# Packed attention and a squared-ReLU layer on one core: values by nine tokens per partition, W_out by four rows per partition

## The chip, the cores and the metric

The kernel runs on one core of a Trainium2 chip. The core's engines run side by side and wait for each other by semaphores: PE (TensorE) does matmuls from the SBUF into the PSUM, DVE (VectorE) and ACT (ScalarE) work on elements of both memories, POOL (GpSimd) works on the SBUF and issues DMAs here, SP (SyncE) issues DMAs. The metric is the device time of one execution in microseconds; lower is better.

## The reference

Inputs are q, k and v of 8 batches x 8 heads x 576 tokens x 64, packed queries p of 32 tokens per head, W_in of 512x2048 and W_out of 2048x512, all float32.

```python
def sm_attn(qq, kk, vv):
    s = scale * np.matmul(qq, kk.transpose(0, 1, 3, 2))
    s = s - np.max(s, axis=-1, keepdims=True)
    a = np.exp(s)
    a = a / (np.sum(a, axis=-1, keepdims=True) + 1e-09)
    return np.matmul(a, vv)
p_packed = sm_attn(p, k, v)                  # 32 packed tokens per head
out = sm_attn(q, p_packed, p_packed)         # back to 576 tokens per head
x = out.transpose(0, 2, 1, 3).reshape(B * S, H * D)
h = x @ w_in
g = np.maximum(h, 0.0) ** 2
return g @ w_out                             # 4608 x 512
```

## The kernel before

**The work.** Each batch is done in two attention steps and two layers. The 8 heads of a batch are two groups of four (qd 0 and 1), each with 4 x 32 = 128 packed tokens on the partitions. First attention: scores `s1` of the 32 packed tokens of each head against 576 keys, negative maximum `m1` on DVE, exponential `x1` with its sums on ACT into `e1` (128 x 576 per group), turned by PE (`eT`) in pieces of 128 columns into PSUM, copied out (`eo`), and multiplied with the values (`pv`). `rd` and `pp` divide by the sums, `pt`/`po` and `bd`/`bs` turn the result. Second attention: scores `s2`, turned (`t2`), maximum `m2`, subtraction `sb`, exponential `x2`, sums `su`, division `a2`, turned (`aT`) to `a2T`. As the values of the second attention are the packed result, W_in is multiplied by it first: `w0` to `w3` give the product with W_in for one batch in four quarters of 512 columns, copied from PSUM by `W0` to `W3` into the tile `wp`. Then come the layers: `h` multiplies one block of 128 hidden features with half of a batch's tokens (288 columns, two matmuls; batches 0 and 1 are cut into 256 and 320), `r` is the ReLU from PSUM, `q` the square of two blocks into `gT`, `o` two of the 16 matmuls of 128 tokens by 512 columns with W_out, `c` the copy of a finished tile of 128 tokens to the SBUF, `d` its store.

**The order.** All of it stands in one string, ORDER, whose words are issued one after the other: `h3.0.11` is batch 3, half 0, block 11; `r3.0.11:a` its ReLU on ACT (`:v` DVE, `:p` POOL, DVE where nothing stands); `o12.4` the fifth pair of tile 12; `eT41` batch 4, group 1; `Lk`, `Lv`, `Lq` load keys, values and queries, `Wi` and `Wo` the weights. Each engine takes its own words in this order and waits only for the results and buffers that it needs. So the place of a DVE word among PE words means nothing by itself; its place among DVE words does. Loads of inputs and weights are issued by POOL, stores by SP, each queue in order of its words.

**Buffers around the change.** [...] A bank comes free when its ReLU or copy is done. `e1` is a single buffer for both groups. Finished tiles have five buffers (`op`); a buffer comes free when its store is done.

**What the change touches** (lines of the profile). `setup` (L192 to L195) makes three value buffers `v_b` and two `v_end`, the latter cleared. For batches 2 to 7 `load_v` (L313 to L320) issues two DMAs per group: 512 tokens, four neighbouring tokens per partition, into `v_b`; and the 64 that are left into one half of the partitions of `v_end`. `st_exp1` (L439) writes `e1` in the order of the tokens. `st_e1T` (L461) turns four pieces of every fourth column per group, and in group 1 a fifth with the last 64 tokens of group 0 and the first 64 of group 1. `st_pv` (L488) multiplies: per batch four matmuls for that fifth piece, with 128 columns (L500), and 32 with 64 columns (L507), all with 128 rows and 32 columns of the array. Batches 0 and 1 have another form (three tokens per row piece, 96 rows) and keep it. `load_w_out` (L263) loads a quarter of W_out so that partition p of block fb holds row 128 fb + p. `st_wp_out` (L626) copies a quarter of `wp` with its columns in order.

Of the kernel before, what the change touches and what calls it, by code (L numbers as in the profile page):

```python
# [12 lines left out]
BF16 = mybir.dt.bfloat16  # L13
# [55 lines left out]
h1.1.12 r1.1.0:a bd2 pt2 qT20 o4.7 bs2:a Lk40 h1.1.5 po2:v r1.1.12:a o5.7 q1.1.0:v c4:a h1.1.10 r1.1.5:v c5:a s22 d4
r1.1.10:v h1.1.4 o6.0 t221 r1.1.4:a h1.1.9 d5 o7.0 q1.1.2:a t220 h1.1.13 r1.1.9:a o6.1 qT30 r1.1.13:a Lq4 h1.1.11  # L70
q1.1.4:a m221 w22 w32 r1.1.11:a o6.2 m220 W32:a h1.1.14 h1.1.15 W22:v Lv31 o6.3 r1.1.14:a q1.1.6:a o7.1 o6.4 sb21:v
r1.1.15:a Lv40 o7.2 q1.1.5:a kT30 o7.3 q1.1.7:a o7.4 sb20:v Lk41 x221 o6.5 qT31 o7.5 x220 o6.6 su21 o6.7 o7.6 su20 c6:a
o7.7 w02 a221:v c7:a d6 w12 o8.0 W02:a a220:v o8.1 d7 o8.2 aT21 W12:a o8.3 aT20 o8.4 Lq5 h2.0.1 h2.0.0 r2.0.1:v o8.5
r2.0.0:a o8.6 q2.0.0:v h2.0.2 h2.0.3 r2.0.2:v o9.0 Lk50 o8.7 r2.0.3:v h2.0.5 c8:a s13 q2.0.1:v r2.0.5:a h2.0.4 d8 m130
o10.0 r2.0.4:a h2.0.6 kT40 h2.0.7 r2.0.6:a o10.1 r2.0.7:a q2.0.2:v h2.0.10 Lk51 x130 m131 o9.1 h2.0.8 r2.0.10:a q2.0.3:v
o9.2 r2.0.8:a kT41 h2.0.13 x131 eT30 h2.0.9 r2.0.13:v o10.2 eo30:a rd3 r2.0.9:v h2.1.1 eT31 q2.0.4:v h2.0.14 r2.1.1:a
o10.3 r2.0.14:v eo31:a h2.0.11 Lk61 o9.3 r2.0.11:v o9.4 h2.0.12 h2.1.5 q2.0.5:v r2.0.12:a pv3 r2.1.5:v h2.0.15 q2.0.6:v
h2.1.4 pp3 r2.0.15:a o9.5 r2.1.4:v h2.1.6 bd3 pt3 q2.0.7:v h2.1.0 bs3:a o9.6 r2.1.6:v r2.1.0:v Lv41 po3:a o9.7 q2.1.2:v
h2.1.8 q2.1.0:v c9:a h2.1.2 r2.1.8:v s23 r2.1.2:a Lv50 d9 o11.0 t230 h2.1.3 h2.1.7 t231 o10.4 r2.1.3:a w23 m230 r2.1.7:a
w03 W23:a h2.1.10 q2.1.1:v h2.1.9 q2.1.3:v o10.5 W03:a m231 o10.6 o11.1 sb30:v r2.1.10:a o11.2 r2.1.9:a sb31:v o10.7  # L80
x230 o11.3 q2.1.4:v c10:a h2.1.15 qT40 o11.4 x231 h2.1.11 su30 r2.1.15:a w13 d10 r2.1.11:a w33 W13:a h2.1.14 su31
h2.1.13 o12.0 r2.1.14:a a230:v o12.1 r2.1.13:a o12.2 W33:a q2.1.5:v o12.3 a231:v h2.1.12 o11.5 aT30 r2.1.12:a o12.4 aT31
o12.5 q2.1.6:v q2.1.7:v h3.0.5 h3.0.2 qT41 r3.0.5:a o12.6 h3.0.0 r3.0.2:v Lq6 o11.6 r3.0.0:a o12.7 h3.0.1 h3.1.1
r3.0.1:v c12:a o11.7 r3.1.1:v s14 d12 c11:a q3.0.0:v h3.0.4 kT50 h3.0.3 r3.0.4:a o13.0 r3.0.3:a m140 d11 h3.0.9 Lk60
o14.0 r3.0.9:a q3.0.1:v h3.1.3 x140 kT51 h3.1.0 o14.1 r3.1.3:a m141 o13.1 Lk70 r3.1.0:a h3.0.8 q3.0.2:v eT40 x141 h3.0.7
r3.0.8:v o13.2 eo40:v r3.0.7:a h3.0.6 q3.1.0:v o14.2 q3.0.4:v r3.0.6:a eT41 rd4 q3.0.3:v h3.0.11 eo41:a h3.1.2 r3.0.11:v
o14.3 r3.1.2:v o13.3 h3.0.12 h3.0.10 q3.1.1:v pv4 r3.0.10:a r3.0.12:v o14.4 Lv51 pp4 h3.0.13 q3.0.5:v h3.0.14 r3.0.13:a
bd4 o13.4 r3.0.14:v bs4:a pt4 Lv60 q3.0.6:v h3.0.15 h3.1.8 o13.5 po4:v r3.1.8:a o14.5 r3.0.15:v s24 q3.0.7:v h3.1.11
t240 h3.1.6 r3.1.11:a o13.6 t241 r3.1.6:a o13.7 w04 qT51 c13:a w14 h3.1.4 W04:a m241 o16.0 d13 h3.1.5 m240 r3.1.4:a
o16.1 r3.1.5:a o14.6 W14:a sb41:v h3.1.9 h3.1.7 q3.1.2:v o14.7 r3.1.7:a sb40:v r3.1.9:a w24 w34 x241 q3.1.3:v h3.1.10  # L90
c14:v o16.2 W34:a h3.1.13 q3.1.4:v d14 o15.0 su41 r3.1.10:a o16.3 x240 o15.1 r3.1.13:v W24:a h3.1.12 q3.1.5:v o16.4
a241:v o15.2 r3.1.12:a h3.1.14 su40 h3.1.15 o16.5 r3.1.14:a q3.1.6:v o15.3 r3.1.15:a a240:v o15.4 o16.6 q3.1.7:v o15.5
aT40 aT41 o16.7 qT50 o15.6 c16:a h4.0.1 h4.0.4 Lq7 r4.0.1:v o15.7 d16 r4.0.4:v o17.0 c15:a h4.0.3 h4.0.2 r4.0.3:v o17.1
# [20 lines left out]
r6.0.4:v o26.1 qT70 x171 h6.0.0 h6.0.2 d25 o26.2 r6.0.0:v r6.0.2:a rd7 eT70 q6.0.0:v h6.0.14 eo70:v h6.0.9 r6.0.14:a
o26.3 r6.0.9:v h6.0.5 o27.0 r6.0.5:v h6.0.6 eT71 q6.0.2:v r6.0.6:a h6.0.11 o26.4 eo71:v r6.0.11:a h6.0.3 q6.0.5:v h6.1.1
pv7 r6.1.1:v o26.5 r6.0.3:a pp7 o26.6 q6.0.1:v h6.0.7 bd7 h6.1.5 pt7 o27.1 bs7:v r6.1.5:a r6.0.7:a o26.7 po7:v q6.0.3:v
h6.0.15 c26:a h6.0.8 w07 w27 r6.0.15:v W07:a d26 o28.0 W27:v h6.1.0 o27.2 r6.0.8:a r6.1.0:a o28.1 q6.0.7:v o27.3
q6.0.4:v q6.1.0:v h6.0.12 h6.1.6 r6.0.12:v o28.2 o28.3 r6.1.6:v h6.0.13 o27.4 h6.1.7 r6.0.13:v s27 r6.1.7:a o27.5
# [16 lines left out]
class Kernel:  # L135
# [42 lines left out]
    def setup(self):  # L178
# [15 lines left out]
        for x in self.v_end:  # L194
            nc.vector.memset(x, 0.0)  # L195
# [673 lines left out]
```

## Time and profile before

| | |
|---|---|
| median of three runs | 240.62 us (240.46 to 240.88) |
| the profiled execution | 240.85 us, of which 239.1 us are the span from the first to the last instruction |
| busy, share of the span | PE 230.8 us (97%), DVE 200.4 (84%), ACT 143.9 (60%), POOL 73.0 (31%) |
| DMA | 28.50 MB in 31868 packets, 119 GB/s over the span |

Times are in microseconds, means of one instruction in nanoseconds. A row of a group gives line, engine, operation, output and inputs, shapes and count; behind the first bar the busy time and the mean of one instruction; behind the second the engine's idle time just before these instructions and what ended it. PE's instructions overlap: a matmul's duration includes its way through the array, and the next starts before it ends, so what one costs in a row of equal ones is the distance of their starts. The chain is followed back from the last instruction, at each step to what released it; its shares add up to the span. A window's row has one column per engine: busy time and number of instructions, then the granted clock of TensorE and the DMA's share. A row of waits names who waited for whom, the sum, the number of waits and the longest.

### The profile page before, as it was taken

To read this page: it belongs to the slowest core of one execution; us is meant where nothing else is said; L and a number is where in the kernel's file an instruction comes from. 1 tells how busy PE (TensorE), PEld (TensorE's weight loads), DVE (VectorE), ACT (ScalarE), POOL (GpSimd) and SP (SyncE) were. 2 spreads that over 40 slices of the span, in tenths; PEclk is the share of its full clock that TensorE was granted. 3 is DMA by queue.
4 is the path that set the end of the run, shared out by engine and by line. 5 is a ranking of instruction groups with operands and counts; after the bars stand their busy time and mean duration, and the time that the engine had idled before them with its cause. 6 is when DMAs were issued, how large, how long until landed. Compare 5 with 4: busy or idle time off the path is not lost.

```text
span 239.1 us, 5971 instructions
## 1 busy us (share of the span) xinstructions
PE 230.8 (97%) x2355; PEld 123.5 (52%) x2355; DVE 200.4 (84%) x455; ACT 143.9 (60%) x311; POOL 73.0 (31%) x122
## 2 busy tenths in 40 slices
PE   8887999999999999999999999999999999999994
PEld 2444553456544564456545654565545644555543
DVE  2779986998997889989998889997899789987740
ACT  2348974887896657775683648774485346732300
POOL 8509782785664661054203340002000000000000
PEclk9999999999999999999999999999999999999999
DMA  6999999999999979169923993216112112111224
GB/s 109 193 200 213 200 206 204 161 243 211 199 203 217 192 106 143 44 91 197 127 64 45 195 129 60 47 44 96 45 27 67 47 44 46 44 47 44 49 59 111
DMA packets 31868, 28.50 MB, mean 119 GB/s; under 512 B 8161, under 2 KB 26337, under 8 KB 31841
## 3 DMA queue, kind: packets, MB, share of 16 engines
q0 software_dynamic: 25312, 18.55, 53.7%
q1 hardware_dynamic: 6384, 9.51, 14.9%
q8 instruction: 18, 0.29, 0.5%
q10 hardware_dynamic: 144, 0.07, 0.1%
q14 instruction: 10, 0.07, 0.1%
HBM read 37.22 MB, written 9.44 MB: 195 GB/s over the span
## 4 chain that ended last, share of the span: by engine, by line
PE 92%; DVE 5%; ACT 1%; issue 0%; ACTq 0%
PE ps_o L694 52%; PE ps_h L637 26%; PE ps_s L411 3%; PE ps_wp L623 3%; PE ps_idle L341 3%; PE ps_e1T L474 2%; PE ps_pv L507 1%; DVE r L644 1%; DVE sums L591 1%; ACT qT L457 1%; DVE wp L459 0%; PE ps_pv L500 0%; DVE a2T L613 0%; DVE gT L682 0%; DVE s L563 0%; PE ps_o L699 0%
## 5 line engine op out<-in xcount | busy, mean ns | idle before, releaser
L694 PE MATMUL ps_o<-w_out_bf,gT 128*128 128x512 bf16 (+1 forms) x576 | 147.0, 378 | 0.0
L637 PE MATMUL ps_h<-a2T,wp 128*128 128x288 bf16 (+2 forms) x512 | 89.9, 286 | 1.5 <-ACT wp L457 0.7
L642 ACT ACTIVATE r<-ps_h 128x288 bf16<-128x288 f32 (+2 forms) x161 | 61.4, 413 | 48.7 <-PE ps_h L637 44.0
L694 PEld LDWEIGHTS <-gT 128*128 128x128 bf16 x576 | 54.5, 98 | 43.9 <-issue 3.4
L637 PEld LDWEIGHTS <-wp 128*128 128x128 bf16 x512 | 47.5, 98 | 42.8 <-issue 7.7
L644 DVE TENSOR_SCALAR r<-ps_h 128x288 bf16<-128x288 f32 (+2 forms) x95 | 41.3, 449 | 11.8 <-PE ps_h L637 10.7
L682 DVE TENSOR_TENSOR gT<-r 128x576 bf16<-128x576 bf16 (+2 forms) x108 | 46.5, 444 | 2.3 <-ACT r L642 1.4
L457 ACT CAST wp<-ps_wp 128x1024 bf16<-128x1024 f32 (+1 forms) x31 | 29.2, 961 | 9.1 <-PE ps_wp L623 9.1
L457 ACT COPY o_sb<-ps_o 128x512 f32<-128x512 f32 x26 | 15.2, 590 | 12.3 <-PE ps_o L694 12.0
L271 POOL DMA_DIRECT2D q_b<-in_q_dram x16 | 10.9, 685 | 29.1 <-DVE qT L369 25.2
L319 POOL DMA_DIRECT2D v_b<-in_v_dram x12 | 9.3, 779 | 32.3 <-PE ps_pv L507 30.4
L271 POOL DMA_DIRECT2D k_b<-in_k_dram x28 | 15.3, 550 | 12.1 <-DVE kT L357 5.0
L451 ACT ACTIVATE e<-ps_s,nm 128x576 bf16<-128x576 f32 x16 | 11.8, 743 | 7.1 <-DVE nm L437 7.1
L357 DVE STREAM_TRANSPOSE kT<-k_b 128x576 uint32<-128x576 uint32 x16 | 12.3, 770 | 2.9 <-DMA k_b<-in_k_dram 2.9
L341 PE MATMUL ps_idle<-gT 128*128 128x512 bf16 (+1 forms) x34 | 11.4, 465 | 1.2 <-DVE gT L190 1.2
L437 DVE TENSOR_REDUCE nm<-ps_s 128x1 f32<-128x576 f32 x16 | 11.5, 740 | 1.1 <-PE ps_s L411 1.1
L369 DVE STREAM_TRANSPOSE qT<-q_b 128x576 uint32<-128x576 uint32 (+2 forms) x16 | 10.8, 683 | 2.0 <-DMA q_b<-in_q_dram 2.0
L680 ACT ACTIVATE gT<-r 128x640 bf16<-128x640 bf16 (+1 forms) x18 | 12.2, 694 | 0.4 <-DVE r L644 0.2
L591 DVE TENSOR_REDUCE sums<-e 128x18 f32<-128x576 f32 (+2 forms) x20 | 12.1, 604 | 0.0
L585 ACT ACTIVATE e<-d 128x576 f32<-128x576 f32 (+2 forms) x20 | 11.7, 600 | 0.6 <-DVE d L579 0.6
L579 DVE TENSOR_TENSOR d<-s,mx 128x576 f32<-128x576 f32 (+2 forms) x19 | 11.7, 641 | 0.0
L573 DVE TENSOR_REDUCE mx<-s 128x18 f32<-128x576 f32 (+2 forms) x20 | 11.6, 609 | 0.0
(68 smaller groups left out, 175.5 us busy)
## 6 DMA issues: line engine op xcount, KB each, us to landing
out_dram<-o_sb SPq DMA_DIRECT2D x65, 128.0 KB, 2.4
v_b<-in_v_dram POOLq DMA_DIRECT2D x12, 256.0 KB, 5.6
w_out_bf<-in_moe_w_out_dram POOLq DMA_DIRECT2D x4, 512.0 KB, 10.7
q_b<-in_q_dram POOLq DMA_DIRECT2D x6, 288.0 KB, 6.2
q_b<-in_q_dram POOLq DMA_DIRECT2D x12, 144.0 KB, 6.9
k_b<-in_k_dram POOLq DMA_DIRECT2D x12, 108.0 KB, 4.7
gT<-in_v_dram POOLq DMA_DIRECT2D x4, 288.0 KB, 7.9
w_in_bf<-in_moe_w_in_dram POOLq DMA_DIRECT2D x4, 256.0 KB, 10.7
```

The costliest lines, as they stand in the source:

```text
L271: engine.dma_start(x[n:], s[:P - n])
L341: self.nc.tensor.matmul(ps[:, :m], lhsT=self.nought[:, :P], rhs=self.nought[:, :m], start=True, stop=True)
L357: self.nc.vector.transpose(t["kT"][:].rearrange("p s e -> p (s e)").bitcast(U32), t["k"][:].rearrange("p t d -> p (t d)").bitcast(U32))
L451: self.nc.scalar.activation(out, x, ACT.Exp, bias=t["nm"], accum_out=self.den[b][:, qd:qd + 1])
L457: engine.copy(out, x)
L591: nc.vector.reduce_sum(out=sums[:, x], in_=t["e2"][:, x], axis=AX.X)
L637: self.nc.tensor.matmul(ps, lhsT=self.att[b, 0]["wp"][:, qd, fb * P:(fb + 1) * P], rhs=self.att[b, qd]["a2T"][:, s0:s1], start=(qd == 0), ...
L642: engine.activation(r, ps, ACT.Relu)
L644: engine.tensor_scalar_max(r, ps, 0.0)
L680: engine.activation(out, r, ACT.Square)
L682: engine.tensor_tensor(out=out, in0=r, in1=r, op=ALU.mult)
L694: self.nc.tensor.matmul(self.o[tt][:, e], lhsT=self.gT[:, fb, a:a + P], rhs=self.w_out_bf[:, fb, e], start=(i == 0), stop=(i == self.NFB - 1))
```

## The change

Three things change, for batches 2 to 7 where nothing else is said.

- **Values.** Tokens go nine per partition: group 0's four heads lie on partitions 0 to 63, group 1's on 64 to 127, loaded by one DMA per group into one of two buffers (by the batch's parity). The exponentials of both groups are written into one row of 9 x 128 columns, so that piece j holds, for both groups, the tokens 9p + j; one exponential thereby writes every second column. `eT` of group 0 turns pieces 0 to 4, that of group 1 pieces 5 to 8, and each piece holds both groups. `pv_tiles` does 72 matmuls per batch on tiles of 64 rows and 32 columns, the two groups into two PSUM banks. `v_end` and its clearing go.
- **W_out.** Each quarter is loaded with four neighbouring rows per partition. Hidden features are permuted to match: the copy of `wp` from PSUM reads every fourth column, for all batches.
- **The order.** From the twelfth `h` of batch 1 on the same words stand in another order, and part of them on another engine: squares 59 on DVE and 49 on ACT (98 and 10 before), ReLUs 71 and 142 (81 and 132), W copies 4 and 20 (2 and 22), `bs` 4 and 2 (2 and 4). Loads and stores are issued in another order too.

```diff
-        self.v_b = [self.consts.tile([P, QH, 4, D], BF16, name=f"v_b{i}") for i in range(3)]
-        self.v_end = [self.consts.tile([P, QH, self.NQ, D], BF16, name=f"v_end{i}") for i in range(2)]
-        for x in self.v_end:
-            nc.vector.memset(x, 0.0)
+        self.v_b = [self.consts.tile([P, QH, T // 2, D], BF16, name=f"v_b{i}") for i in range(2)]
...
-            self.w_out_bf[:, f0:f1, :], self.w_out[f0 * P:f1 * P].rearrange("(fb p) e -> p fb e", p=P))
+            self.w_out_bf[:, f0:f1, :], self.w_out[f0 * P:f1 * P].rearrange("(p fb) e -> p fb e", p=P))
...
-        o, r = (D, 0) if qd else (0, 4 * P)
-        self.nc.gpsimd.dma_start(x, s[:, o:o + 4 * P].rearrange("h (p j) d -> p h j d", j=4))
-        self.nc.gpsimd.dma_start(y[qd * D:(qd + 1) * D, :, qd, :], s[:, r:r + D].rearrange("h p d -> p h d"))
+        x = t["v"] = self.v_b[b % 2][qd * D:(qd + 1) * D]
+        self.nc.gpsimd.dma_start(x, s.rearrange("h (p j) d -> p h j d", j=T // 2))
...
-            out = e1.rearrange("p (l a u) -> p l a u", a=2, u=T // 2)
-            x = t["ps_s1"][:, :, :HALF].rearrange("p a (u l) -> p l a u", l=NP)
+            out = self.e1[b][:].rearrange("p (u q l a) -> p q a u l", q=self.NQ, l=NP, a=2)[:, qd]
+            x = t["ps_s1"][:, :, :HALF].rearrange("p a (u l) -> p a u l", l=NP)
...
-            x = [t["e1"][:, o + j:o + 4 * P:4] for j in range(4)]
-            if qd:
-                x.append(self.e1[b][:].rearrange("p q s -> p (q s)")[:, 4 * P:5 * P])
+        n, cuts = (3, (0, 6, 12)) if b in THREES else (QH, (0, 5, 9))
+        x = [self.e1[b][:, j * n * NP:(j + 1) * n * NP] for j in range(cuts[qd], cuts[qd + 1])]
...
+    def pv_tiles(self, b):
+        quads = range(self.NQ)
+        ps = self.turn32("ps_pv")[:, :, :D]
+        for qd in quads:
+            self.att[b, qd]["ps_pv"] = ps
+        n = T // 2
+        for j in range(n):
+            e1T = self.att[b, j // 5]["e1T"][:, j % 5]
+            for h in range(QH):
+                g = slice(NP * h, NP * h + NP)
+                for qd in quads:
+                    t = self.att[b, qd]
+                    self.nc.tensor.matmul(t["ps_pv"][g, qd], lhsT=e1T[qd * D:(qd + 1) * D, g], rhs=t["v"][:, h, j, :],
+                                          start=(j == 0), stop=(j == n - 1))
...
-        x = slice(None) if qd is None else qd
-        self.copy(engine, wp[:, x, f:f + self.NE], t["ps_wp", n][:, x, :])
+        x = slice(None) if qd is None else slice(qd, qd + 1)
+        self.copy(engine, wp[:, x, f:f + self.NE].rearrange("p q (j c) -> p q j c", c=P),
+                  t["ps_wp", n][:, x, :].rearrange("p q (c j) -> p q j c", c=P))
```

Of the new order, the stretches around the exponentials of batch 2, around `pv4`, and the loads and last stores as the queues of POOL and SP see them:

```
Lk30 h1.0.11 q1.0.4:v s12 r1.0.12:a r1.0.11:v q1.0.5:a m121 h1.1.1 h1.0.13 o5.3 o4.3 r1.0.13:v h1.0.14 r1.1.1:a x121
r1.0.14:a h1.0.15 m120 o5.4 r1.0.15:v x120 o4.4 kT31 q1.0.6:v h1.1.7 r1.1.7:a h1.1.2 rd2 eT20 eT21 h1.1.6 r1.1.2:a o5.5
...
x141 r3.0.0:v q3.0.0:v x140 d4 q2.1.3:v Lk50 h3.0.9 o12.2 eT40 r3.0.3:a r3.0.9:v qT41 h3.0.6 q2.1.6:a h3.0.2 r3.0.6:a
o11.3 o11.4 eT41 r3.0.2:a h3.0.11 eo40:a d10 h3.0.8 rd4 qT40 eo41:v r3.0.11:v pv4
...
POOL: Lk30 Lv30 Lq3 Lq4 Lk41 Lk61 Lk40 Lv31 Lq5 Lv40 Lv41 Lk50 Lq7 Lv50 Lv51 Lk51 Lq6 Lk60 Lv60 Lk71 Lk70 Lv61 Lv71 Lv70
SP: ... d26 d23 d28 d27 d24 d30 d16 d29 d32 d25 d31 d33 d34 d35
```

More of the change, by code (lines that the diff above doesn't have):

```diff
@@ L69 @@
[L69 to L93, printed above, removed]
@@ L114 @@
[L114 to L118, printed above, removed]
@@ new lines @@
+o12.0 h3.0.1 o11.0 q2.1.4:a o11.1 q2.1.7:a m140 d9 m141 r3.0.1:a h3.0.0 o12.1 r3.0.4:a h3.0.3 q2.1.5:v o11.2 x141
+r3.0.0:v q3.0.0:v x140 d4 q2.1.3:v Lk50 h3.0.9 o12.2 eT40 r3.0.3:a r3.0.9:v qT41 h3.0.6 q2.1.6:a h3.0.2 r3.0.6:a o11.3
+o11.4 eT41 r3.0.2:a h3.0.11 eo40:a d10 h3.0.8 rd4 qT40 eo41:v r3.0.11:v pv4 pp4 Lq7 o11.5 bd4 q3.0.1:a h3.1.1 bs4:v kT50
+pt4 r3.0.8:a h3.0.14 o12.3 r3.1.1:a po4:v h3.0.5 r3.0.14:a o11.6 r3.0.5:a h3.0.10 r3.0.10:v q3.0.2:a s24 h3.0.13
+q3.0.4:a o11.7 h3.0.12 t240 r3.0.12:a t241 m240 o12.4 o12.5 r3.0.13:a h3.1.2 Lv50 h3.1.3 o12.6 c11:a sb40:v q3.0.5:v
@@ new lines @@
+Lv51 r3.1.3:a o12.7 h3.0.7 r3.1.2:a h3.1.0 o14.0 o14.1 m241 q3.0.6:v qT50 Lk51 r3.0.7:a q3.1.1:v c12:a x240 h3.1.8 o13.0
+sb41:v o13.1 r3.1.0:a h3.1.6 r3.1.8:a qT51 h3.0.15 w34 r3.1.6:a w14 q3.0.3:v r3.0.15:a h3.1.4 o13.2 su40 h3.1.5 o13.3
+r3.1.4:a h3.1.12 d11 W34:a r3.1.12:v o14.2 r3.1.5:a q3.1.0:v o13.4 h3.1.11 h3.1.15 kT51 W14:a w04 r3.1.15:v x241 su41
+w24 q3.0.7:a o13.5 a240:v h3.1.7 W24:a o14.3 r3.1.7:a o14.4 o13.6 h3.1.13 r3.1.11:a o13.7 W04:a r3.1.13:a q3.1.2:a
+h3.1.10 o14.5 a241:v c13:a Lq6 r3.1.10:v o14.6 h3.1.9 q3.1.3:v aT40 r3.1.9:v q3.1.5:a s15 aT41 h3.1.14 o14.7 Lk60
@@ new lines @@
+h7.1.13 r7.1.13:a h7.1.10 r7.1.10:v o31.3 o31.4 q7.1.6:a h7.0.14 h7.0.15 q7.1.0:v r7.0.15:a o32.3 r7.0.14:v o31.5 o31.6
+h7.1.9 q7.0.7:a h7.1.6 o32.4 r7.1.9:a o31.7 r7.1.6:a o32.5 h7.1.2 h7.1.4 r7.1.2:a r7.1.4:a o32.6 o32.7 c31:v d29 o34.0
+q7.1.1:v c32:v d32 h7.1.11 d25 h7.1.7 o34.1 q7.1.2:a r7.1.7:a r7.1.11:a o33.0 h7.1.8 q7.1.3:a d31 o33.1 o34.2 r7.1.8:v
+h7.1.14 q7.1.4:a h7.1.15 o33.2 o34.3 o33.3 q7.1.5:v o33.4 r7.1.14:a r7.1.15:a o34.4 q7.1.7:v o33.5 o33.6 o33.7 o34.5
+c33:a o34.6 o34.7 o35.0 o35.1 o35.2 o35.3 c34:v o35.4 o35.5 o35.6 d33 d34 o35.7 c35 d35
@@ L173, in __init__ @@
         self.att, self.den, self.r, self.o, self.o_sb, self.ph = {}, {}, {}, {}, {}, {}
-        self.stage, self.open, self.loaded_v = -1, {}, 0
+        self.stage, self.open = -1, {}
         self.engines = {"v": self.nc.vector, "a": self.nc.scalar, "p": self.nc.gpsimd}
@@ L312, in load_v @@
             return
-        x = self.v_b[self.loaded_v % len(self.v_b)]
-        self.loaded_v += 1
-        y = self.v_end[b % len(self.v_end)]
-        t["v"] = [x[:, :, j, :] for j in range(4)]
-        t["v_end"] = y
-        o, r = (D, 0) if qd else (0, 4 * P)
-        self.nc.gpsimd.dma_start(x, s[:, o:o + 4 * P].rearrange("h (p j) d -> p h j d", j=4))
-        self.nc.gpsimd.dma_start(y[qd * D:(qd + 1) * D, :, qd, :], s[:, r:r + D].rearrange("h p d -> p h d"))
+        x = t["v"] = self.v_b[b % 2][qd * D:(qd + 1) * D]
+        self.nc.gpsimd.dma_start(x, s.rearrange("h (p j) d -> p h j d", j=T // 2))
     def group(self, qd, h):
@@ L440, in st_exp1 @@
         if b not in self.e1:
-            self.e1[b] = self.one.tile([P, self.NQ, S], BF16, name="e1")
-        e1 = self.e1[b][:, qd]
+            self.e1[b] = self.one.tile([P, self.NQ * S], BF16, name="e1")
         if b not in self.den:
@@ L490, in st_pv @@
         n = len(qds)
-        if b in THREES:
-            ps = self.bank32(b, "ps_pv", n)
-        else:
-            ps = self.turn32("ps_pv")[:, 0, :n * D].rearrange("p (q d) -> p q d", d=D)
-        m = range(len(self.att[b, qds[0]]["v"]))
-        if b not in THREES:
-            t = self.att[b, qds[-1]]
-            for h in range(QH):
-                g = NP * h
-                self.nc.tensor.matmul(ps[g:g + NP, :, :D], lhsT=t["e1T"][:, m[-1] + 1, g:g + NP],
-                                      rhs=t["v_end"][:, h], start=True, stop=False)
+        if b not in THREES:
+            self.pv_tiles(b)
+            return
+        ps = self.bank32(b, "ps_pv", n)
+        m = range(6)
         for j, i in [(j, i) for j in m for i in range(n)] if b else [(j, i) for i in range(n) for j in m]:
@@ L507, in st_pv @@
                 self.nc.tensor.matmul(ps[g:g + NP, i, :D], lhsT=t["e1T"][:, j, g:g + NP],
-                                      rhs=t["v"][j][:, h, :], start=(j == 0 and b in THREES), stop=(j == m[-1] and (i == n - 1 or b in THREES)))
+                                      rhs=t["v"][j][:, h, :], start=(j == 0), stop=(j == m[-1]))
+    def pv_tiles(self, b):
[12 more added lines that the diff above has]
+                                          start=(j == 0), stop=(j == n - 1))
     def st_pp(self, b, *qds):
```

98 lines of the change are left out of this document (53 added, 45 removed).

## The prediction

> **What bounds the kernel now.** I read the page first (busy shares, the chain that ended last), then the chain and the busy time by stage between 54 and 236 us, then what PE's weight loads wait for there.
>
> ```profile
> span 239.1 us, 5971 instructions
> ...
> PE 230.8 (97%) x2355; PEld 123.5 (52%) x2355; DVE 200.4 (84%) x455; ACT 143.9 (60%) x311; POOL 73.0 (31%) x122
> ...
> PE 92%; DVE 5%; ACT 1%; issue 0%; ACTq 0%
> ```
> ```profile
> by line: PE ps_o L694 59.6%; PE ps_h L637 30.2%; PE ps_wp L623 3.7%; PE ps_s L411 2.7%; PE ps_e1T L474 1.7%; PE ps_pv L507 0.8%; PE ps_pv L500 0.6%; PE ps_o L699 0.5%; PE ps_ppT L544 0.2%; ACT o_sb L707 0.1%; issue 0.0%; ACTq L707 0.0%
> ```
> ```profile
> core 0: us, PE busy (x) PEld busy (x) DVE busy (x) ACT busy (x) POOL busy (x), PEclk, DMA share, GB/s
> 54.00:236.00 182.00, 181.75 (x1795) 98.55 (x1793) 158.40 (x346) 109.59 (x239) 38.68 (x65) 1.00 0.56 98
> ...
> 90.00:120.00 30.00, 30.00 (x342) 15.88 (x339) 27.92 (x61) 21.51 (x47) 8.40 (x14) 1.00 0.77 123
> ```
> ```profile
> PEld L694 <- DVE gT L682: 0.8, 4, 0.2
> PEld L623 <- DVE gT L682: 0.2, 1, 0.2
> PEld L474 <- ACT e L451: 0.2, 1, 0.2
> ```
>
> The second line is the chain for 54 to 236 us alone, the stretch in which the two orders differ: apart from the last copy it is PE all the way, 108 us of output matmuls and 55 us of hidden-layer matmuls of 182. PE is busy 181.75 of 182 us at a granted clock of 1.00. A busy PE need not run at its best, so I check the pace:
>
> ```profile
> 67.00 0.56 PE ps_wp L623 x16
> ...
> 68.63 5.18 PE ps_o L694 x24
> ...
> 184.09 0.49 PE ps_h L637 x4
> ```
>
> 24 output matmuls of 512 columns take 5.18 us, 216 ns each, and 4 hidden matmuls of 288 columns 0.49 us, 122 ns each: 0.42 ns per column in both, so nothing is lost between them. The weight loads' waits for a result add up to 1.2 us, and that is all that a better order can give back here. DVE is behind PE but near it (158 of 182 us, 27.9 of 30 where it is densest), ACT far from it (110). So a change can gain only by taking PE instructions away or by touching the first 26 us, and it can lose wherever a result comes later than PE asks for it.
>
> **The change part by part.** Durations from here on are of these rows.
>
> ```profile
> L642 ACT ACTIVATE r<-ps_h 128x288 bf16<-128x288 f32 x121 | 46.8, 414 | 44.8 <-PE ps_h L637 41.0 <-issue 1.8 <-DVE gT L682 0.8
> L682 DVE TENSOR_TENSOR gT<-r 128x576 bf16<-128x576 bf16 x96 | 41.6, 446 | 2.3 <-ACT r L642 1.4
> L644 DVE TENSOR_SCALAR r<-ps_h 128x288 bf16<-128x288 f32 x71 | 30.9, 449 | 10.0 <-PE ps_h L637 9.4
> L457 ACT CAST wp<-ps_wp 128x1024 bf16<-128x1024 f32 x27 | 26.9, 1018 | 7.6 <-PE ps_wp L623 7.6
> L451 ACT ACTIVATE e<-ps_s,nm 128x576 bf16<-128x576 f32 x16 | 11.8, 743 | 7.1 <-DVE nm L437 7.1
> L437 DVE TENSOR_REDUCE nm<-ps_s 128x1 f32<-128x576 f32 x16 | 11.5, 740 | 1.1 <-PE ps_s L411 1.1
> L369 DVE STREAM_TRANSPOSE qT<-q_b 128x576 uint32<-128x576 uint32 x12 | 9.1, 758 | 0.0
> L599 DVE TENSOR_TENSOR a<-e,rs 128x576 bf16<-128x576 f32 x12 | 9.1, 782 | 0.0
> L579 DVE TENSOR_TENSOR d<-s,mx 128x576 f32<-128x576 f32 x12 | 8.7, 744 | 0.0
> L585 ACT ACTIVATE e<-d 128x576 f32<-128x576 f32 x12 | 8.3, 703 | 0.2 <-DVE d L579 0.2
> L507 PE MATMUL ps_pv<-v_b,e1T 128*32 128x64 bf16 x192 | 2.5, 193 | 0.0
> L319 POOL DMA_DIRECT2D v_b<-in_v_dram x12 | 9.3, 779 | 32.3 <-PE ps_pv L507 30.4 <-DMA w_out_bf<-in_moe_w_out_dram 1.9
> L320 POOL DMA_DIRECT2D v_end<-in_v_dram x12 | 7.7, 639 | 1.9 <-DMA w_out_bf<-in_moe_w_out_dram 1.7 <-issue 0.2
> L474 PE MATMUL ps_e1T<-ident,e 128*128 128x128 bf16 x54 | 5.0, 219 | 0.0
> L680 ACT ACTIVATE gT<-r 128x640 bf16<-128x640 bf16 x10 | 7.2, 747 | 0.0
> L459 DVE CAST wp<-ps_wp 128x1024 bf16<-128x1024 f32 x3 | 3.7, 1217 | 0.4 <-PE ps_wp L623 0.4
> L459 DVE COPY e1T<-ps_e1T 128x512 bf16<-128x512 bf16 x5 | 2.1, 410 | 0.2 <-PE ps_e1T L474 0.2
> ```
>
> *Values times weights, six batches.* Before, a batch takes 4 matmuls with 128 columns (L500) and 32 with 64 (L507), four side by side on 128x32 tiles:
>
> ```profile
> 60.24 0.24 PE L500 MATMUL ps_pv<-v_end,e1T 128*32 128x128 bf16 x4
> 60.25 0.36 PEld L507 LDWEIGHTS <-e1T 128*32 128x32 bf16 x32
> 60.30 0.42 PE L507 MATMUL ps_pv<-v_b,e1T 128*32 128x64 bf16 x32
> ...
> 60.65 0.72 PE L637 MATMUL ps_h<-a2T,wp 128*128 128x320 bf16 x4
> ```
>
> From 60.24 to the next hidden matmul at 60.65 that is 0.41 us of PE's time. One of the 32 lasts 0.19 us, so they start (0.42 - 0.19) / 31 = 7.4 ns apart: 0.03 us for a round of four, about the 27 ns of its 64 columns. After, there are 72 matmuls on 64x32 tiles, 9 rounds if eight run side by side. That they do is seen in W_in times packed rows (L623, also 64x32): 16 of them with 512 columns take 0.56 us, two times 216 ns and an end of 0.13. The replaced rounds are 0.06 (the four wide ones) plus 8 x 0.03 = 0.30 us, the new ones 9 x 0.03 = 0.27: -0.025 us a batch with rounding undone, -0.15 us in six. Bounds: if tiles of the two row halves took turns, 72 x 7.4 ns = 0.53 us, +0.23 a batch and +1.4 in all; below, -0.25.
>
> *Exponentials and their turning.* There are nine turns per batch as before, of whole 128-column pieces, so PE's work stays. What moves is the wait: a piece now holds both head groups, so the first turn waits for both exponentials. After the scores (s1) that takes at least two maxima and one exponential, 2 x 0.74 + 0.74 and some 0.2 us for the matmul's end: 2.4 us. Counting PE's words between s1 and the first turn in the new order (0.44 us per o, 0.25 per h) I find 3.2 us of work in batch 2, then 3.9, 3.8, 4.1, 4.7 and 6.6. Relus and squares that stand between on the two engines eat some of the difference, most in batch 2 (one square of 0.7 and relus of 0.4). I take 0, with 0 to +0.6. The exponential writes every second element now, and reads in order. On DVE the multiplication that writes every second element (L599, 782) stands 38 ns above the subtraction that does not (L579, 744); a like 5% on ACT costs nothing, as ACT has time.
>
> *The late order.* The same words stand from the twelfth h of batch 1 on, in another sequence. Counted by engine: 39 squares and 10 relus go from DVE to ACT, two W copies and two small shifts from ACT to DVE. DVE loses 39 x 0.446 + 10 x 0.449 - 2 x 1.217 - 0.4 = 19 us of 158, ACT gains 39 x about 0.7 + 10 x 0.414 - 2 x 1.018 - 0.6 = 29 us on 110. Both end near 139 of 182 us, so DVE no longer works at 90% behind a PE that never rests. What PE's loads wait for (1.2 us) should shrink; I take -0.3, between 0 and -1.2. I also looked for the tightest places, each as PE's time between giving an input and needing the result, against the work on the engine between. Two hidden banks are reused after 0.66 to 0.68 us of PE work in 27 places before, in 4 after. One place is worse: in batch 4, pv4 stands two h (0.49 us) behind the second turn eT41, while its copy takes 0.41 and the matmul's end (219 less the 55 ns of its 128 columns) and two hand-overs about 0.22. That is +0.14 us if DVE is free; a query transpose (0.758) stands ahead of that copy on DVE, so up to +0.9. I take +0.15. Queue order: stores leave in another sequence, some much later (d25 behind d29), with never more than five tiles held; a copy waits for the store that held its buffer, and that store was issued over 3 us ahead in each place but c27, where it is about 4 us behind c26, and a store lands in 2.4 us (last row of the next fence). Nothing for that.
>
> *Value loads.* Two issues on POOL (0.78 + 0.64 us) become one with as many runs as the second (256), about 0.65 us, and half the descriptors. POOL is busy 31%, and none of it is on the chain. On POOL's queue a load now waits for the turned queries of two batches before (Lq7, Lq6), with value loads behind; each of those has over 15 us left. The key load Lk51 behind them has the least, by my count 2 us before it is turned and 7 before the scores that need it.
>
> ```profile
> v_b<-in_v_dram POOLq DMA_DIRECT2D x12, 256.0 KB, 5.6
> ...
> out_dram<-o_sb SPq DMA_DIRECT2D x65, 128.0 KB, 2.4
> ```
>
> A landing is 5.6 us; the shortest lead, in batch 4, is about 8 us behind both issues even by the position in the order. Nothing on the path.
>
> *W_out and its copies.* The load has longer runs; no PE wait names W_out, so 0. The price is in the W copies, which now read PSUM at every fourth element. Most run on ACT beside other work. One is on the chain, the third quarter of batch 0 on DVE:
>
> ```profile
> 1.14 0.55 DVE L195 MEMSET v_end<- 128x256 uint32 x2
> 2.90 0.33 DVE L235 TENSOR_SCALAR p_b<-gT 128x128 bf16<-128x128 f32 x1 [1.21 <-DMA gT<-in_p_dram]
> 25.13 1.22 DVE L459 CAST wp<-ps_wp 128x1024 bf16<-128x1024 f32 x1
> ...
> 26.40 1.85 PE L637 MATMUL ps_h<-a2T,wp 128*128 128x256 bf16 x14 [0.58 <-DVE wp L459]
> ```
>
> Whatever this copy takes longer, PE starts later, and nothing takes it up afterwards. The nearest row for a strided PSUM read is the old exponential: it reads at every 32nd element and needs 743 ns, the other exponential, from SBUF in order, 703. 40 ns in 576 elements are 71 in 1024: +0.07 us, with 0 and twice the copy (+1.2) as ends. The two memsets that go (0.55 us) end before 1.7 us, and DVE then waits 1.21 us for a DMA: 0.
>
> **The sum**: -0.15 (values) - 0.30 (late waits) + 0.15 (pv4) + 0.07 (the copy at 25 us) = -0.23 us. The profiled execution took 240.85 us (239.1 of span, 1.75 around), which gives 240.62; it lies 0.23 above the median of 240.62, and for the median the sum gives **240.4**.
>
> **The rivals.** A measurement of this kernel can tell some 0.2%, 0.5 us, from no change; that is the bound for faster and slower.
>
> *Faster.* The waits of PE's loads vanish and pv4 waits for nothing: -0.15 - 0.5 to -1.2, 239.3 to 240.0, likeliest 239.9. For it: the evened load, the longer reuse distances. Against: only 1.2 us is there to be had, and the waits listed overlap matmuls in part.
>
> *Slower by the strided copy.* If DVE needs over 40% longer for every fourth element (1.7 instead of 1.2 us), the copy at 25 us alone costs 0.5 us; at double, 240.4 + 1.1 = 241.5. The row of the old exponential speaks against. [...]
>
> *Slower by the order.* Exponential to turn in batches 2, 4 and 5, or copy to pv in batches 3 to 5, late by 0.2 to 0.9 us each: +0.6 to +2, 241.5. For: the margins above are sums of rows without the wait for a semaphore. Against: the same sums with the old order's margins, which are smaller, left PE without a wait.
>
> *Slower by the tiles.* The row halves take turns: 240.4 + 1.5 = 241.9. Against: L623.
>
> **How the numbers follow.** No measurable change (the sum) 0.42; faster 0.32; strided copy 0.08; order 0.13; tiles 0.05: slower 0.26. The range has to leave out 0.2: below, it takes in most of the faster case (239.7, half of the 1.2 us gone); above, the slower ones up to 241.6. The likeliest case's own range is 240.15 to 241.1.
>
> **What would show it.** Right: the chain from 54 us on is still PE; L507 has 72 matmuls a batch within 0.4 us; ACT about 75%, DVE about 75% of the span; the wait of PE for DVE wp at 25 us is 0.6 to 0.7; pv4 behind eT41 shows one wait of 0.1 to 0.3. Wrong: PE waits over 1 us in all behind 54 us, for r, e or e1T; W copies well above 1.02 (ACT) or 1.22 us (DVE); tiles of values 14 ns apart per pair instead of 7.

## The result and the profile after

| | before | after |
|---|---|---|
| median | 240.56 us (240.46 to 240.88, 6 runs) | 241.84 us (241.73 to 242.62, 6 runs) |
| ratio to before, 95% interval | | 1.0057 (1.0043 to 1.0071) |
| the profiled execution | 240.85 us, span 239.1 | 241.92 us, span 240.1 |
| busy share of the span | PE 97%, DVE 84%, ACT 60%, POOL 31% | PE 95%, DVE 77%, ACT 70%, POOL 26% |

The change costs 1.3 us, 0.6%, and the time lies above the range that was given (239.7 to 241.6). The page of the changed kernel, then its chain of work and its busy times from 54 to 237 us:

```profile
span 240.1 us, 6343 instructions
...
PE 228.2 (95%) x2535; PEld 125.2 (52%) x2571; DVE 185.0 (77%) x410; ACT 167.9 (70%) x354; POOL 63.2 (26%) x110
```
```profile
by line: PE ps_o L687 55.7%; PE ps_h L630 30.0%; PE ps_wp L615 3.7%; PE ps_s L402 2.7%; PE ps_pv L499 2.3%; PE ps_e1T L456 1.6%; issue 1.3%; DMA out_dram<-o_sb 1.2%; SPq L718 1.0%; ACT o_sb L446 0.3%; PE ps_ppT L536 0.3%; ACT o_sb L700 0.1%
```
```profile
54.00:237.00 183.00, 180.72 (x1982) 99.92 (x2008) 143.49 (x302) 133.18 (x281) 29.98 (x53) 1.00 0.52 97
```

The chain is PE up to 232.1 us; its last 4.9 us here run through a copy, three stores and the last copy (more on them under "Stores" below). Of PE's shares one has clearly grown: the products of weights and values (`ps_pv`) were 0.8% and 0.6% of 182 us, 2.5 us, and are 2.3% of 183, 4.2 us. (36 of PE's 2571 matmuls have no record in this trace, all 2571 weight loads have one; shares of single lines are a little low for `ps_o`. The 1.0 us that the trace calls PE's waits for "issue" in front of L687 are six gaps of one missing matmul each.)

Both kernels do the same words in the same order up to a pair of output matmuls at about 53.5 us. From there to the first of the last 16 matmuls the timeline gives the distance. Before:

```profile
53.61 0.59 PE L694 MATMUL ps_o<-w_out_bf,gT 128*128 128x512 bf16 x2
...
234.69 1.06 PE L699 MATMUL ps_o<-w_out_bf,gT 128*128 128x128 bf16 x16
```

After:

```profile
53.41 0.59 PE L687 MATMUL ps_o<-w_out_bf,gT 128*128 128x512 bf16 x2
...
235.82 1.06 PE L692 MATMUL ps_o<-w_out_bf,gT 128*128 128x128 bf16 x16
```

181.08 against 182.41 us: the whole 1.33 us is lost behind 53 us, and the first 53 us are no slower. The place is seen in the timeline around the products of batch 2 (start, length of the group, matmuls in it). Before they began at 60.24 and the next hidden matmul at 60.65. After:

```profile
59.56 0.75 PE L499 MATMUL ps_pv<-v_b,e1T 64*32 64x64 bf16 x72
60.24 0.58 PE L630 MATMUL ps_h<-a2T,wp 128*128 128x320 bf16 x3
```

0.68 us in place of 0.41. Cut off at 59.78, the same view has only 32 of the 72:

```profile
59.56 0.31 PE L499 MATMUL ps_pv<-v_b,e1T 64*32 64x64 bf16 x32
```

One matmul lasts 0.195 us, so the first 32 all start within 0.12 us, eight at a time as the prediction had it. Then none starts for 0.10 us, and the last 40 need until 0.55. In the records of the single instructions the starts are 0, 3, 7, 10, 13, 17, 20, 23 ns, the next eight from 39 on, the 32nd at 122 ns, the 33rd at 227, and then one every 8.33 ns to the 72nd at 552. All six batches show this; batch 5 has a further stop, of 0.16 us, in front of its 65th.

From these records theory A: PE has 32 pairs of weight load and matmul ready when a burst begins and runs them at the array's pace; the 33rd starts about 226 ns behind the first, and from there a pair comes every 8.33 ns, whatever the array could do. Rival B: tiles of 64 rows hinder each other. Rival C: the new order costs the time.

### The profile page after: what moved, and what is told of

The parts are those of the page before. It is cut to its first block, busy times and chain, and to the rows that moved or that the text cites. A ratio compares the mean times of both kernels' runs of the same rounds, so it can differ in the third digit from the quotient of the medians.

```text
span 240.1 us, 6343 instructions
## 1 busy us (share of the span) xinstructions
PE 228.2 (95%) x2535; PEld 125.2 (52%) x2571; DVE 185.0 (77%) x410; ACT 167.9 (70%) x354; POOL 63.2 (26%) x110
## 3 DMA queue, kind: packets, MB, share of 16 engines
q0 software_dynamic: 17440, 18.55, 48.7%
## 4 chain that ended last, share of the span: by engine, by line
PE 85%; DVE 4%; DMA 4%; issue 2%; POOL 1%; ACT 1%; SPq 1%; POOLq 0%
PE ps_o L687 49%; PE ps_h L630 26%; DMA gT<-in_v_dram 3%; PE ps_wp L615 3%; PE ps_s L402 3%; PE ps_pv L499 2%; PE ps_e1T L456 2%; DMA out_dram<-o_sb 1%; SPq L718 1%; DVE r L637 1%; DVE sums L583 1%; ACT qT L446 1%; POOL k_b L268 1%; DVE wp L448 0%; DVE a2T L605 0%
## 5 line engine op out<-in xcount | busy, mean ns | idle before, releaser
L687 PE MATMUL ps_o<-w_out_bf,gT 128*128 128x512 bf16 (+1 forms) x543 | 142.1, 378 | 2.3 <-issue 1.1
L635 ACT ACTIVATE r<-ps_h 128x288 bf16<-128x288 f32 (+2 forms) x171 | 64.8, 412 | 38.4 <-PE ps_h L630 37.6
L687 PEld LDWEIGHTS <-gT 128*128 128x128 bf16 x576 | 54.6, 98 | 42.4 <-issue 4.1
L637 DVE TENSOR_SCALAR r<-ps_h 128x288 bf16<-128x288 f32 (+2 forms) x85 | 37.5, 450 | 22.6 <-PE ps_h L630 20.9
L673 ACT ACTIVATE gT<-r 128x576 bf16<-128x576 bf16 (+2 forms) x57 | 38.8, 689 | 2.1 <-DVE r L637 1.9
L675 DVE TENSOR_TENSOR gT<-r 128x576 bf16<-128x576 bf16 (+2 forms) x69 | 30.0, 443 | 3.2 <-ACT r L635 3.1
L446 ACT CAST wp<-ps_wp 128x1024 bf16<-128x1024 f32 (+1 forms) x29 | 27.4, 958 | 4.9 <-PE ps_wp L615 4.8
L268 POOL DMA_DIRECT2D k_b<-in_k_dram x28 | 15.5, 559 | 12.5 <-DVE gT L675 8.7
L441 ACT ACTIVATE e<-ps_s,nm 128x576 bf16<-128x576 f32 x16 | 13.6, 866 | 7.1 <-DVE nm L428 6.9
L591 DVE TENSOR_TENSOR a<-e,rs 128x576 bf16<-128x576 f32 (+2 forms) x17 | 11.8, 711 | 0.1
L270 POOL DMA_DIRECT2D k_b<-in_k_dram x19 | 10.1, 531 | 6.2 <-DMA q_b<-in_q_dram 4.7
L448 DVE COPY o_sb<-ps_o 128x512 f32<-128x512 f32 x9 | 6.2, 690 | 6.8 <-PE ps_o L687 6.6
```

Of the source, the lines that this page charges most:

```text
L268: engine.dma_start(x[n:], s[:P - n])
L441: self.nc.scalar.activation(out, x, ACT.Exp, bias=t["nm"], accum_out=self.den[b][:, qd:qd + 1])
L446: engine.copy(out, x)
L635: engine.activation(r, ps, ACT.Relu)
L637: engine.tensor_scalar_max(r, ps, 0.0)
L673: engine.activation(out, r, ACT.Square)
```

## The experiments

The last column but one is the distance of the two timelines above for each run's profile, here from weight load to weight load, since no weight load's record is missing: from the second of the pair at 53.5 us to the last of all. It leaves out the first 53 us, which vary from run to run.

| run | ratio to before (95%) | from 53 us on, us | against before |
|---|---|---|---|
| before | | 181.86 | |
| after | 1.0057 (1.0043 to 1.0071) | 183.19 | +1.33 |
| old values in the changed kernel | 0.9999 (0.9981 to 1.0017) | 181.70 | -0.17 |
| new order alone | 1.0004 (0.9981 to 1.0027) | 181.84 | -0.02 |
| W_out alone | 0.9999 (0.9987 to 1.0012) | 181.87 | +0.01 |
| new values alone | 1.0181 (1.0158 to 1.0204) | 186.24 | +4.38 |
| 32 products a batch | 0.9934 (0.9914 to 0.9955) | 180.70 | -1.16 |
| 48 products a batch | 0.9990 (0.9971 to 1.0008) | 181.81 | -0.05 |
| before, cut into 64 pairs | 1.0062 (1.0040 to 1.0084) | 183.33 | +1.47 |
| old values, `pv4` later | 0.9986 (0.9970 to 1.0001) | 181.84 | -0.02 |
| 72 products in two bursts | 1.0069 (1.0048 to 1.0090) | 183.99 | +2.13 |

### The parts of the change, one by one

**The changed kernel with the old values** (order and W_out stay new):

```diff
-        self.v_b = [self.consts.tile([P, QH, T // 2, D], BF16, name=f"v_b{i}") for i in range(2)]
+        self.v_b = [self.consts.tile([P, QH, 4, D], BF16, name=f"v_b{i}") for i in range(3)]
+        self.v_end = [self.consts.tile([P, QH, self.NQ, D], BF16, name=f"v_end{i}") for i in range(2)]
...
-            self.pv_tiles(b)
```

> The changed kernel with the value products of before (four tokens per partition and the padded tile, 36 products a batch); the new order and the new W_out layout stay. Theory A, the burst of 72 products costs it: the burst takes 0.41 us again instead of 0.68, 6 x 0.27 = 1.6 us come back, and 240.1 to 240.4 us is left, 0.2 to 0.4 below the kernel before. Rival C, the new order costs it: the time stays at 241.6 to 242.0 us.

Measured: 240.56 us, ratio 0.9999, a little above the 240.1 to 240.4 expected and far from rival C's 241.6; 1.49 us of the changed kernel's stretch are gone. Rival C falls.

**The new order alone**, the string ORDER of the changed kernel in the kernel before:

> The kernel before with the new order alone (values and W_out as before). Theory A: 240.1 to 240.5 us, the gain of about 0.3 us by the late waits and nothing else, so within 0.2 us of the kernel above. Rival C: 241.5 to 242.0 us.

Measured: 241.02 us with 240.86 for the kernel before beside it, ratio 1.0004. Rival C falls here too, but so does the gain of 0.3 us that I expected: nothing is gained or lost. The records of the single matmuls show why. Late starts between matmuls on the full array fall by 0.34 us, but `pv4` starts 0.165 us late in this order, and W_in's products take 0.12 us more; both are taken up again below.

**W_out alone:**

```diff
-            self.w_out_bf[:, f0:f1, :], self.w_out[f0 * P:f1 * P].rearrange("(fb p) e -> p fb e", p=P))
+            self.w_out_bf[:, f0:f1, :], self.w_out[f0 * P:f1 * P].rearrange("(p fb) e -> p fb e", p=P))
...
-        self.copy(engine, wp[:, x, f:f + self.NE], t["ps_wp", n][:, x, :])
+        self.copy(engine, wp[:, x, f:f + self.NE].rearrange("p q (j c) -> p q j c", c=P),
+                  t["ps_wp", n][:, x, :].rearrange("p q (c j) -> p q j c", c=P))
```

> The kernel before with W_out by four neighbouring rows per partition and the copies of the combined weights to suit, nothing else. Theory A and rival C: within 0.15 us of the kernel before, since the copies took 1019 ns on ACT and 1207 ns on DVE against 1018 and 1217. The rival of the prediction that a copy with strided columns costs time: 0.3 to 1.0 us above the kernel before.

Measured: 240.76 us, ratio 0.9999. Strided copies cost nothing; the rows of the changed kernel say the same. In the groups of ACT and DVE, and in PE's waits between 20 and 30 us:

```profile
L446 ACT CAST wp<-ps_wp 128x1024 bf16<-128x1024 f32 x25 | 25.2, 1019 | 3.6 <-PE ps_wp L615 3.5
```
```profile
L448 DVE CAST wp<-ps_wp 128x1024 bf16<-128x1024 f32 x5 | 6.0, 1207 | 0.0
```
```profile
PE ps_h L630 <- DVE wp L448: 0.6, 1, 0.6
```

**The new values alone**, in the old order but for one pair of words:

```diff
-eT40 x141
+x141 eT40
```

> The kernel before with the new values alone (its own order but for one pair of steps in batch 4 changed about, its own W_out). Theory A: 6 x 0.27 = 1.6 us above the kernel before, 241.9 to 242.4 us, with a burst of 0.66 to 0.70 us a batch. Rival C: 240.4 to 240.7 us.

Measured: 244.96 us, ratio 1.0181. The burst is 680 ns as expected, and that is 1.6 us; but 4.4 us are lost. The rest is a wait that the changed kernel does not have. PE's waits from 40 us on and one of the places in the timelines of PE and ACT:

```profile
PE ps_e1T L456 <- ACT e L441: 2.0, 3, 0.9
```
```profile
84.96 0.41 PE L629 MATMUL ps_h<-a2T,wp 128*128 128x288 bf16 x2
86.10 0.45 PE L456 MATMUL ps_e1T<-ident,e 128*128 128x128 bf16 x5 [0.73 <-ACT e L441]
```
```profile
83.66 0.91 ACT L441 ACTIVATE e<-ps_s,nm 128x576 bf16<-128x576 f32 x1
84.41 0.20 ACT L441 ACTIVATION_READ_ACCUMULATOR e<-ps_s,nm 128x1 f32 x1
84.50 0.72 ACT L634 ACTIVATE r<-ps_h 128x288 bf16<-128x288 f32 x2
85.08 0.92 ACT L441 ACTIVATE e<-ps_s,nm 128x576 bf16<-128x576 f32 x1
```

The first turn needs both exponentials, and the second, which stands behind a ReLU on ACT, ends at 86.00. PE starts 0.54, 0.89, 1.03 and 0.13 us late in four batches, 2.6 us together; with the bursts that makes 4.2 of the 4.38. So the new order is not idle in the changed kernel: it covers these waits, which the old values never had.

### The number of pairs

**Four of the nine pieces of the values** (in the two runs that follow, part of the sum over tokens is left out):

```diff
-        n = T // 2
+        n = 4
```

> The changed kernel with four of the nine pieces of the values multiplied (five are left out of the sum), 32 products of 64x32 a batch in place of 72. Theory A, 32 pairs of weight load and product start at 8 per 29 ns and those after them at 8.33 ns: from the first product to the next other matmul 0.24 to 0.30 us in place of 0.68, so 6 x 0.40 = 2.4 us less than the changed kernel, 239.2 to 239.7 us. Rival B, tiles of 64x32 take turns and cost the same at each place of the burst: 0.68 x 32/72 = 0.30 us for the products alone with the fixed part on top, about 0.38 us, 1.8 us less, 239.9 to 240.2 us, and the spacing of the first 32 as slow as that of the others.

Measured: 239.18 us, just below the 239.2 to 239.7 expected. With 32 products the burst is as long as the first 32 of the 72 were, and the next matmul starts 243 ns behind the first:

```profile
59.33 0.31 PE L499 MATMUL ps_pv<-v_b,e1T 64*32 64x64 bf16 x32
59.57 0.84 PE L630 MATMUL ps_h<-a2T,wp 128*128 128x320 bf16 x4
```

**Six of the nine pieces** (n = 6):

> The changed kernel with six of the nine pieces of the values multiplied (three are left out of the sum), 48 products a batch. Theory A: 24 pairs fewer at 8.33 ns each, 0.68 - 0.20 = 0.48 us a burst, 1.2 us less than the changed kernel, 240.4 to 240.8 us. The first 32 start in about 122 ns, then a pause, then 8.3 ns each. Rival B: 0.68 x 48/72 = 0.45 us at one even pace.

Measured: 240.22 us with 240.58 before beside it; the time is a little below the 240.4 to 240.8 expected, the burst is as expected, 481 ns:

```profile
59.61 0.55 PE L499 MATMUL ps_pv<-v_b,e1T 64*32 64x64 bf16 x48
60.09 0.72 PE L630 MATMUL ps_h<-a2T,wp 128*128 128x320 bf16 x4
```

Lengths of the groups of 32, 48 and 72 products are 0.31, 0.55 and 0.75 us: 8.3 ns for each of the last 24, and 16 more behind the 32nd cost 0.24, that is 16 times 8.3 ns and the pause of 0.10. An even pace (rival B) does not give these three.

**The kernel before with narrower products**, its own tiles of 128x32 and the same columns in all:

```diff
-            for h in range(QH):
-                g = NP * h
-                self.nc.tensor.matmul(ps[g:g + NP, i, :D], ...
+            for h in range(QH):
+                g = NP * h
+                last = j == m[-1] and i == n - 1
+                for c in (slice(0, D),) if b in THREES or last else (slice(0, D // 2), slice(D // 2, D)):
+                    self.nc.tensor.matmul(ps[g:g + NP, i, c], ...
```

> The kernel before with 28 of its 32 narrow value products of a batch cut into two of 32 columns each: 4 wide and 60 narrow pairs, 64 in place of 36, all on tiles of 128x32 as before, and the same sums. Theory A, the number of pairs alone counts: 28 pairs more at 8.33 ns, 0.41 + 0.23 = 0.64 us a burst and 6 x 0.23 = 1.4 us slower than the kernel before, 241.8 to 242.1 us. Rival B, the tiles of 64x32 cost it: the same columns in all on the same tiles, 0.41 to 0.45 us a burst, at most 0.2 us slower.

Measured: 242.18 us, ratio 1.0062, as slow as the changed kernel without one tile of 64 rows. From 60.11 to the next hidden matmul it is 0.66 us:

```profile
60.11 0.24 PE L500 MATMUL ps_pv<-v_end,e1T 128*32 128x128 bf16 x4
60.18 0.66 PE L509 MATMUL ps_pv<-v_b,e1T 128*32 128x32 bf16 x60
60.77 0.72 PE L639 MATMUL ps_h<-a2T,wp 128*128 128x320 bf16 x4
```

So the number of pairs costs it, on these tiles too. That 28 x 8.33 ns, the reckoning of theory A, meets the measured 0.24 us is in part luck: four products of 32 columns start 25 ns apart here, against 29 for four of 64, so 15 rounds in place of 8 already cost some 0.14 us by these starts. The rest comes behind the 33rd pair, where two weight loads start every 16.7 ns, 8.33 each. This pace, and the eight 64x32 products in 29 ns at the start of each burst of the changed kernel, decide against rival B.

**The 72 products in two bursts** of 32 and 40 with a pair of other matmuls between:

```diff
-pv2 r1.1.4:a q1.1.3:a qT21 h1.1.3 pp2
+pv2 r1.1.4:a q1.1.3:a qT21 h1.1.3 pw2 pp2
...
-            self.pv_tiles(b)
+            self.pv_tiles(b, 0, 4)
...
+            "pw": lambda: self.pv_tiles(b, 4, T // 2),
```

> The changed kernel with its 72 products a batch in two bursts, 32 and 40, and a pair of hidden or output matmuls between them (0.24 to 0.43 us). Theory A, PE holds 32 pairs ahead of time and is then supplied at 8.33 ns a pair: each burst starts its first 32 in about 122 ns, the second one needs a further 227 - 122 + 7 x 8.33 ns for its last eight; first to next matmul 243 ns and 227 + 58 + 129 = 414 ns in place of 681, with one more lead-in of 0.09 us: 0.07 us a batch more, +0.4 us, 242.1 to 242.5. Rival D, something that is not refilled in 0.4 us (a limit per accumulation or of PSUM, not of the supply): the second burst runs at 8.33 ns from its first pair on, 40 x 8.33 + 129 = 462 ns, +0.7 us.

Measured: 242.57 us, just above the 242.1 to 242.5 expected. (The lead-in of the expectation: the first product of a burst starts 0.216 us behind a hidden matmul of 288 columns, where a matmul on the full array follows after 0.122.) Batch 2 in the timeline:

```profile
60.07 0.31 PE L499 MATMUL ps_pv<-v_b,e1T 64*32 64x64 bf16 x32
60.32 0.45 PE L630 MATMUL ps_h<-a2T,wp 128*128 128x320 bf16 x2
60.69 0.48 PE L499 MATMUL ps_pv<-v_b,e1T 64*32 64x64 bf16 x40
61.11 0.45 PE L630 MATMUL ps_h<-a2T,wp 128*128 128x320 bf16 x2
```

Burst by burst it is what theory A says, 243 and 414 ns; in the records of the single instructions the second burst starts its first 32 in 122 ns again, and its 33rd 227 ns behind its first. So after 0.37 us of other matmuls 32 pairs start at the first pace again, and rival D falls. In time the cut costs 0.8 us from 53 us on, 0.4 more than worked out. Most of that lies outside the bursts: the turn of the result (L536) now follows the second burst by two other matmuls and waits for `pp4` on DVE, and starts 0.27 us late in batch 4 and 0.06 in batch 6. (A gap of 0.23 us in front of the second burst of batch 7 is no wait: one of the two output matmuls there has no record, and both weight loads have one.)

### The margin in front of `pv4`

**The old values in the new order, a pair of output matmuls moved:**

```diff
-r3.0.11:v pv4 pp4 Lq7 o11.5 bd4
+r3.0.11:v o11.5 pv4 pp4 Lq7 bd4
```

> The new order and the new W_out with the value products of before, as in the run of that kind, and one pair of output matmuls put ahead of the products of batch 4. There the first product started 381 ns behind the last hidden matmul instead of 216, waiting for the copy of the turned exponentials; 0.43 us of other work in between covers it. Expected: that gap is 216 ns again, the stretch from the first step that both orders share to the last matmul falls from 181.7 to 181.5 us, and the time is 240.1 to 240.5, 0.1 to 0.4 below the kernel before. If the copy's lateness moves along (it waits for what the pair frees), 181.7 and 240.2 to 240.7.

Measured: 240.56 us, ratio 0.9986 (0.9970 to 1.0001); the stretch is 181.84 against 181.70, so the gain failed to come. The wait in front of `pv4` is gone, but the moved pair had covered another. PE in the run without the move, then with it:

```profile
102.75 0.65 PE L638 MATMUL ps_h<-a2T,wp 128*128 128x288 bf16 x4
103.50 0.24 PE L500 MATMUL ps_pv<-v_end,e1T 128*32 128x128 bf16 x4
```
```profile
102.85 0.42 PE L507 MATMUL ps_pv<-v_b,e1T 128*32 128x64 bf16 x32
103.20 0.42 PE L638 MATMUL ps_h<-a2T,wp 128*128 128x288 bf16 x2
103.72 0.23 PE L544 MATMUL ps_ppT<-ident,pp 128*128 128x128 bf16 x1
```

The turn of the result (L544) now follows the products by one hidden block, waits for `pp4` on DVE, and starts 0.26 us late; 0.165 had been gained. None of the kernels that do the whole sum beats the kernel before by more than its measurement can tell.

## Why the prediction was wrong, point by point

**Values times weights: this step failed.** It says "the new ones 9 x 0.03 = 0.27" and -0.15 us in six batches; measured are 0.68 us a batch. Five batches lost 0.266 us each, the sixth, which is followed by W_in products, 0.147: +1.48 us where -0.15 was forecast. The inference from L623 was right as far as it went: eight tiles do run side by side. But its 16 matmuls are fewer than the 32 that start at that pace (the 32nd 122 ns behind the first), and 72 are more; a row with few instructions says nothing of the rate at which many are supplied. The profile of before had a row that would have said it, the products of batch 1:

```profile
33.53 0.56 PE L507 MATMUL ps_pv<-gT,e1T 96*32 96x64 bf16 x48
34.02 0.45 PE L637 MATMUL ps_h<-a2T,wp 128*128 128x320 bf16 x2
```

There the array needs 29 ns for four (the records of the first 32), and the weight loads of the last 15 come every 8.3 ns, 33 ns for four: hardly visible with four tiles side by side, and over twice the array's time with eight (67 ns against 29). The rival "the tiles take turns" gave 241.9, next to the 241.84 measured, with 0.05 of the chances, but by luck: its mechanism is refuted by the first 32 products, of which eight start in 29 ns.

What the runs show is the number 32, the 33rd pair 225 to 227 ns behind the first on tiles of 64x32, and 8.33 ns a pair from there on. That PE holds 32 pairs ready ahead of time is the author's reading of these starts; it fits all the bursts, the refilled one too, but for the stop in batch 5. What sets the number and the pace no run shows, nor whether pairs or instructions are counted, as every pair here has two.

**Late waits: the term came, but the order has a price that was not in the sum.** Between neighbouring matmuls on the full array, ten places in the kernel before start over 25 ns later than usual (216 ns behind 512 columns, 122 behind 288), 0.53 us together; in the changed kernel there is one, of 0.04. That is -0.49 us, more than the -0.30 forecast; the bound of 1.2 us was made of waits of weight loads, and the matmuls themselves started only 0.53 us late. What was not in the sum: the order separates two W_in quarters that ran as one group of 16, and two groups of 8 cost 0.12 us more than one of 16, beside the products and all; and in batch 5 the burst is 0.17 us longer, with the stop at its 65th pair, for which the trace names no cause. With the bursts that is 1.48 + 0.12 + 0.17 - 0.49 = 1.28 of the 1.33 us; another 0.03 passes in the W_in products behind the last burst.

**`pv4` behind eT41: right in place, wrong for this kernel.** With the old values, whose first product needs the second turn, the new order has PE start 0.165 us late there (381 ns behind the matmul ahead, 216 elsewhere), almost the 0.15 expected. With the new values only pieces 5 to 8 need it, from the 41st pair on, 0.29 us into the burst: no wait.

**Exponentials: 0 was right, for the reason named.** No wait of PE for them is left behind 54 us. The strided write was dearer than I took it, not 5% but 22%:

```profile
L441 ACT ACTIVATE e<-ps_s,nm 128x576 bf16<-128x576 f32 x16 | 13.6, 866 | 7.1 <-DVE nm L428 6.9
```

The mean of this row takes in the four exponentials of batches 0 and 1, which are as before (742 to 751 ns). The twelve that write every second element take 897 to 921, 907 in the mean, against 742 for the same twelve before. ACT had time for it in the new order; the run with the new values alone shows the price without that cover.

**DVE and ACT:** forecast were about 139 us each from 54 us on, measured 143.5 and 133.2. What relieving DVE can be worth is bounded by the late starts above: from 53 us on no more than 0.53 us was there to be had, however much work leaves DVE.

**W copies:** +0.07 expected, 0 measured (1019 ns against 1018 on ACT, 1207 against 1217 on DVE). A copy over 40% longer, or twice as long, as the rival by the strided copy supposed, no run shows. **Value loads:** hidden, as expected; a load of both parts in one lands in 6.6 us, and POOL is at 26%. "Half the descriptors" was a miscount, without effect: the 512 and 256 runs of the two issues became 256, a third and not half (with the longer runs of W_out, the packets of queue q0 on the page fell from 25312 to 17440).

**Stores:** "Nothing for that" holds for the time, not for the waits. At the end all five tiles are taken, and the last two copies wait for a store; the changed kernel's waits from 225 us on:

```profile
ACT o_sb L700 <- DMA out_dram<-o_sb: 4.2, 1, 4.2
...
DVE o_sb L699 <- DMA out_dram<-o_sb: 1.9, 1, 1.9
```

The copy on ACT starts at 236.91, 0.25 us behind the start of PE's last matmul, before 0.30: the store landed just as PE was done, and the wait took no time from the end.

## What to carry to other kernels

When a change multiplies small instructions, count them before counting columns: here a burst costs the array's time only up to 32 pairs of weight load and matmul, and 8.33 ns a pair behind the 33rd. A pace may be carried over only from a row with as many instructions in a burst, or from the end of a longer one. And a relieved engine or an undone wait is worth no more than the late starts that it causes on the engine that bounds the kernel; and a word moved into one gap may open the gap that it filled, as the pair in front of `pv4` did.

## What the runs showed of the hardware

- The 33rd pair of a burst starts 225 to 227 ns behind the first on 64x32 tiles, and 0.37 us of other work restores the 32. Neighbours on different tiles start 3.3 ns apart. Four products of 32 columns on 128x32 tiles start 25 ns apart, four of 64 columns 29.
- Reading PSUM at every fourth float costs neither ACT (1019 ns against 1018) nor DVE (1207 against 1217) anything; writing every second bf16 element cost ACT's exponential about 165 ns on 742.
- The pair at 53.5 us starts between 53.2 and 54.8 us in the profiles of these kernels, though all do the same words up to there. The first 53 us vary by more than the change is worth, which is why short stretches of the trace tell more here than the times.
